# Normalising the last query block: one product that spreads each head's sum to all its rows, chunk by chunk, in place of a reciprocal of 16 columns, a transpose and four picking products

## The chip, the core and the metric

The kernel runs on one core of one Trainium2 chip. The core has five engines with a queue of instructions each: PE (TensorE, the matrix products), DVE (VectorE), ACT (ScalarE), POOL (GpSimd) and SP (SyncE, which here only issues transfers). They work beside each other and wait for one another through semaphores. The metric is the device time of one execution in microseconds (us), the median of several runs.

## What is computed

The input `A_x` has 2048 rows of 640 numbers. Two attention blocks, A and B, read the same input with weights of their own, and a sigmoid gate mixes their results row by row:

```
x = A_x
g = _sigmoid((x * gate_w).sum(-1, keepdims=True))
a = _A_ref(x, A_wqkv, A_wo)
b = _B_ref(x, B_wqkv, B_wo)
return g * a + (1 - g) * b
```

Each block projects x to queries, keys and values of 32 heads with 20 features each, takes the softmax of the scaled scores of 2048 queries against 2048 keys, weighs the values with it, and multiplies the 640 features with `wo`. What matters here is the last step of a softmax: the weighted values of each head and query have to be divided by that head's and query's sum of exponentials.

## The kernel before, in words

The heads are taken in groups of four, so there are 16 groups (8 of each attention block). For each group the 2048 queries are taken in 4 query blocks of 512, and for each query block the keys in 8 units of two times 128. That makes 512 steps, the loop at L1175. One step computes the scores of 128 keys by 512 queries for each of four heads (`scores`, L672), the exponentials of these on ACT (L675), and the products of the exponentials with the values, which add up in one PSUM bank, `acc` (`values`, L690). Beside that, a step carries products for the row maxima of later units (L614), projections, and the output product of features that are finished (`out_tiles`, L407 through `mms`).

Head h of the four has rows 32h to 32h+20 of `acc`: 20 rows of weighted values, and as row 32h+20 the sum, because the value tile has a column of ones (`DH` is 20). The columns of `acc` are the 512 queries. All other rows are zero, since `acc` is cleared once at the start (L867).

When the 8 units of a query block are done, `take_acc` (L773) empties `acc`, with transposes on DVE, a reciprocal of 16 columns, a product on POOL, and a split of the result into a half-precision part and a half-precision rest. It does this for 63 of the 64 query blocks, while PE goes on with the next one. The change does not touch it.

The last query block of the last group has nothing behind it. It is emptied by `take_last` (L811), called at L1214 after the loop. Before the change it goes like this:

1. ACT copies `acc` (128 rows by 512 queries) to a tile `ot` in SBUF (L814).
2. PE makes four products of 128 queries each (L818), with `ot` as the weights and four columns of the identity as the data: the sums come out turned, with queries as rows, in 16 columns of a PSUM bank.
3. DVE takes the reciprocal of these 16 columns (L820).
4. PE transposes them (L823), so that they have queries as columns, 16 rows of 128. ACT copies these to a tile `rt` (L825).
5. PE makes four more products (L829), with the tile `picks[0]` as the weights: each chooses the four rows of its 128 queries and repeats each over 32 rows. `picks[0]` was built by POOL in the last steps of the loop (`last_picks`, L805, L809).
6. For each of the four chunks of 128 queries, DVE multiplies `ot` by the reciprocals (L834), ACT casts the product to half precision (L835), and POOL takes the rest of it (L836).

Then `last_tiles` (L843) runs for the last query block, called at L1220. For each of the four chunks, and for each half of the 640 output columns, PE makes three products of 320 columns (L854): the half-precision part with the upper and the lower part of the weights, and the rest with the upper part. So there are 24 products in 8 groups of three. The groups of the first half, and both of the last chunk, are scaled and added to the output sums by DVE (L861). The second halves of chunks 0 to 2 are scaled by ACT (L857) and added by POOL (L858). Each chunk is then stored (L863), by SP's queue for chunks 0 and 2 and by ACT's queue for chunks 1 and 3.

What sets the order: the program is written under `tc.manual_schedule()`, so that each engine gets its instructions in the order in which the Python code issues them. `take` and `give` choose PSUM banks by a planned time at which each comes free (`spend`, `tick_block`); that plan chooses banks and moves nothing else here.

Of the kernel before, what the change touches and what calls it, by code (L numbers as in the profile page):

```python
# [11 lines left out]
F32 = mybir.dt.float32  # L12
I32 = mybir.dt.int32
AF = mybir.ActivationFunctionType
OP = mybir.AluOpType
# [4 lines left out]
P = 128  # L20
# [3 lines left out]
DH = 20  # L24
# [5 lines left out]
QB = 512  # L30
# [41 lines left out]
def kernel(  # L72
# [10 lines left out]
    nc = tc.nc  # L83
# [5 lines left out]
    wts = ctx.enter_context(tc.tile_pool(name="wts", bufs=2))  # L89
# [4 lines left out]
    ident = consts.tile([P, P], F32, name="ident")  # L94
# [15 lines left out]
    acc = psum.tile([P, QB], F32, name="acc")  # L110
# [24 lines left out]
    def take():  # L135

        i = min((k for k in range(NB) if k not in held), key=lambda k: free_at[k])
        held.add(i)
        return i, banks[i]

    def spend(engine, cost, ready=0.0):

        clock[engine] = max(clock[engine], ready) + cost
        return clock[engine] + T_BACK

    def give(i, t):
        free_at[i] = t
        held.discard(i)
# [93 lines left out]
    def scales_qk(i, maxima):  # L242

        return scales_by_dram(maxima, 2, lambda r, inv: set_qk(i, r, inv))
# [342 lines left out]
    def unit_of(u):  # L587
        gq, i = divmod(u, NS)
        g, qb = divmod(gq, NQ)
        return g, qb, i  # L590
# [212 lines left out]
    picks = []  # L803

    def last_picks():  # L805

        t = work.tile([P, QB], F32, name="fs")
        picks.append(t[:16].rearrange("p (k e) -> p k e", e=32))
        nc.gpsimd.tensor_copy(picks[0], ident[:16, :16].unsqueeze(2).to_broadcast([16, 16, 32]))  # L809

    def take_last():  # L811

        ot = work.tile([P, QB], F32, name="ot", bufs=2)
        nc.scalar.activation(ot, acc, AF.Copy)  # L814
        i, pt = take()
        one = ident.rearrange("p (h e) -> p h e", e=32)[:, :, DH]
        for t in range(4):
            nc.tensor.matmul(pt[:, 4 * t:4 * t + 4], ot[:, t * P:(t + 1) * P], one, start=True, stop=True)  # L818
        rc = work.tile([P, 16], F32, name="sq", bufs=2)
        nc.vector.reciprocal(rc, pt[:, :16])  # L820
        give(i, spend("dve", 0.3))
        i, pt = take()
        nc.tensor.transpose(pt[:16, :P], rc, ident)  # L823
        rt = wts.tile([16, P], F32, name="rt", tag="rt", bufs=1)
        nc.scalar.activation(rt, pt[:16, :P], AF.Copy)  # L825
        give(i, spend("act", 0.3))
        i, pt = take()
        for t in range(4):
            nc.tensor.matmul(pt[:, t * P:(t + 1) * P], picks[0].rearrange("p k e -> p (k e)")[:, t * P:(t + 1) * P], rt,  # L829
                             start=True, stop=True)  # L830
        o = work.tile([P, 2, QB], F16, name="on", bufs=2)
        for t in range(4):
            c = slice(t * P, (t + 1) * P)
            nc.vector.tensor_tensor(ot[:, c], ot[:, c], pt[:, c], op=OP.mult)  # L834
            nc.scalar.activation(o[:, 0, c], ot[:, c], AF.Copy)  # L835
            nc.gpsimd.tensor_tensor(o[:, 1, c], ot[:, c], o[:, 0, c], op=OP.subtract)  # L836
        give(i, spend("dve", 1.2, spend("act", T_EXP)))
        return o
# [30 lines left out]
    start = start_stack.enter_context(tc.tile_pool(name="start", bufs=1))  # L869
# [60 lines left out]
    for f in drains:  # L930
# [7 lines left out]
                            op=OP.subtract)  # L938
# [97 lines left out]
    work = ctx.enter_context(tc.tile_pool(name="work", bufs=2))  # L1036
# [18 lines left out]
    for g in range(2 * NG):  # L1055
        b = g * step
        n = g + 1
        if n < 2 * NG:
# [5 lines left out]
            i = g // 4 + 1  # L1064
            if i < 4:
                if g % 4 == 0:
                    z, c0 = i // 2, 320 * (i % 2)
                    srcs = max_tasks([[(wqkv[z], part * D + c0 + 160 * k) for k in range(2)] for part in range(2)],
                                     lambda m, i=i: scales_qk(i, m))
# [16 lines left out]
    for z in range(2):  # L1086
        parts = max_tasks([[(wo[z], 160 * k) for k in range(4)]], lambda m, z=z: scales_o(z, m), wrow[z])
        tasks(OMAX[z], 1, parts)
        for i in range(4):
            tasks(OSPLIT[z] + 3 * i, 2, out_weights(z, i))  # L1090
    at((2 * NG - 1) * step + 9, last_weights)
    at(STEPS - 4, last_picks)


# [80 lines left out]
    for G in range(STEPS + 1):  # L1175
        g, qb, i = unit_of(G)
# [12 lines left out]
        for what in (STEP[blocks] if maxima or some else LATE + " X" * (blocks == 2)).split():  # L1189
            k = count[what] = count.get(what, 0) + 1  # L1190
# [21 lines left out]
            else:  # L1212
                slot(G)
    end_o = take_last()  # L1214
    while side or parked or fill or current or outs or last:
        advance()
# [32 lines left out]
```

## Time and profile before

| what | value |
|---|---|
| device time, median of 3 runs | 2765.46 us (2764.1 to 2766.71) |
| device time of the profiled execution | 2765.39 us |
| its span (first to last event of the core) | 2763.6 us |
| mean granted clock of PE | 0.996 of full speed |
| busy time of ACT | 2525.4 us (91%) |
| busy time of DVE | 2441.0 us (88%) |
| busy time of POOL | 671.5 us (24%) |

The profile comes from one execution. Times in it are counted from the start of the span. A row of the timeline has its start, the time from its start to the end of the last instruction that it merges, the engine, the line of the code, the operation, what it writes and reads, the shapes (partitions by elements, type), how many instructions the row merges, and in brackets how long the engine sat idle before it and what ended that. PE counts matrix products, PEld the loading of their weights. A product of 32-bit numbers shows as two products and two loads in the trace. ACTq and SPq are transfers issued from the queues of ACT and SP. The chain of waits is followed back from the last work of the span.

### The profile page before, as it was taken

How to read it: one execution, taken by the hardware profiler on the slowest of the kernel's cores; microseconds unless marked ns; L12 is line 12 of the kernel's file. 1: busy time of each engine (PE TensorE's matmuls, PEld its weight loads, DVE VectorE, ACT ScalarE, POOL GpSimd, SP SyncE). 2: the span in 40 equal slices, each digit the busy share in tenths (PEclk: the TensorE clock that was granted, in tenths of full speed). 3: DMA queues.
4: the chain of work that ended last, by engine and by line, in shares of the span. 5: the costliest groups of instructions: out<-in, count | busy, mean ns of one | idle time of the engine just before them, and what ended most of it. 6: DMA issues, size and time to landing. Idle time of an engine off the chain costs nothing.

```text
span 2763.6 us, 62604 instructions
## 1 busy us (share of the span) xinstructions
PE 2725.5 (99%) x23453; PEld 938.0 (34%) x23453; DVE 2441.0 (88%) x4780; ACT 2525.4 (91%) x5140; POOL 671.5 (24%) x914
## 2 busy tenths in 40 slices
PE   7999999999999999999999999999999999999998
PEld 3433333333333332333333333333333333333222
DVE  7789999999999889888888998989988898999982
ACT  4999999999999999999999899999999999999997
POOL 6322223222123422311222111222342202100111
PEclk8999999999999999999999999999999999999999
DMA  4021102010120212102012230221201112122112
GB/s 142 17 57 26 31 11 47 8 31 16 25 55 20 60 35 56 41 9 61 20 41 66 60 84 26 60 56 48 65 16 42 30 50 63 32 77 64 47 47 76
DMA packets 176433, 125.60 MB, mean 45 GB/s; under 512 B 105216, under 2 KB 145976, under 8 KB 176128
## 3 DMA queue, kind: packets, MB, share of 16 engines
q1 hardware_dynamic: 173584, 119.99, 17.0%
q8 instruction: 183, 3.00, 0.5%
q0 software_dynamic: 1600, 0.96, 0.2%
q14 instruction: 122, 1.00, 0.1%
q10 hardware_dynamic: 944, 0.66, 0.1%
HBM read 55.53 MB, written 31.86 MB: 32 GB/s over the span
## 4 chain that ended last, share of the span: by engine, by line
PE 93%; DVE 4%; ACT 1%; DMA 1%; issue 0%; POOL 0%; SPq 0%; POOLq 0%; DVEq 0%; ACTq 0%
PE acc L690 35%; PE bank L407 20%; PE bank L614 20%; PE bank L672 18%; DVE mpart L625 2%; ACT pt L675 1%; DMA ws<-in_A_wqkv_dram 0%; DVE rl L622 0%; PE bank L854 0%; DVE ot L777 0%; DMA xs<-in_A_x_dram 0%; PE bank L900 0%; ACT rl L618 0%; DVE wmax L258 0%; DMA kd<-dd 0%
## 5 line engine op out<-in xcount | busy, mean ns | idle before, releaser
L675 ACT ACTIVATE pt<-bank 128x512 f32<-128x512 f32 x4096 | 2173.2, 615 | 147.9 <-PE bank L672 105.3
L625 DVE TENSOR_REDUCE mpart<-bank 128x1 f32<-128x512 f32 x2944 | 1842.4, 681 | 220.7 <-PE bank L614 117.4
L690 PE MATMUL acc<-pt,v 128*21 128x512 f32 x8192 | 1081.7, 600 | 0.7 <-DVE ot L777 0.6
L672 PE MATMUL bank<-qt,kt 64*128 64x512 f16 x4096 | 1039.1, 380 | 4.7 <-DVE mpart L625 2.7
L614 PE MATMUL bank<-kt,qt 60*128 60x512 f16 x3520 | 1010.6, 381 | 3.6 <-DVE mpart L625 1.0
L614 PEld LDWEIGHTS <-qt 60*128 60x128 f16 x4096 | 237.9, 94 | 906.8 <-issue 846.1
L622 DVE CUSTOM_DVE_ANT_0 rl<-bank,rl 128x512 f32<-128x512 f32 x576 | 386.7, 677 | 13.3 <-ACT rl L618 8.6
L618 ACT ACTIVATE rl<-bank 128x512 f32<-128x512 f32 x576 | 339.6, 600 | 11.9 <-PE bank L614 11.3
L407 PE MATMUL bank<-xx,wbh 128*128 128x168 f16 (+7 forms) x2600 | 291.4, 234 | 1.5 <-DVE wbh L926 1.0
L672 PEld LDWEIGHTS <-kt 64*128 64x128 f16 x4096 | 229.2, 94 | 178.8 <-issue 69.9
L690 PEld LDWEIGHTS acc<-pt,v 128*21 128x21 f32 x8192 | 143.0, 99 | 426.2 <-issue 421.9
L407 PE MATMUL bank<-xx,wbl 128*128 128x168 f16 (+7 forms) x1300 | 259.9, 232 | 0.0
L785 POOL TENSOR_TENSOR ot<-ot,sq 128x512 f32<-128x512 f32 x63 | 66.0, 1047 | 736.7 <-DVE sq L782 718.1
L407 PEld LDWEIGHTS <-wbh 128*128 128x128 f16 x2600 | 196.5, 98 | 118.4 <-issue 112.7
L614 PE MATMUL bank<-kd,qt 60*128 60x512 f16 x576 | 204.3, 380 | 2.3 <-DMA kd<-dd 2.2
L436 POOL CAST cq<-fs 128x512 f16<-128x512 f32 x60 | 36.6, 610 | 500.8 <-ACT fs L434 500.8
L407 PE MATMUL bank<-woh,o_in 128*128 128x320 f16 (+3 forms) x700 | 157.7, 290 | 0.0
L407 PE MATMUL bank<-wvh,xx 128*128 128x160 f16 (+1 forms) x1280 | 156.0, 234 | 0.0
L407 PEld LDWEIGHTS <-xx 128*128 128x128 f16 x1920 | 131.3, 97 | 56.1 <-issue 53.8
L407 PE MATMUL bank<-wvl,xx 128*128 128x160 f16 (+1 forms) x640 | 137.6, 232 | 0.0
L407 PEld LDWEIGHTS <-wbl 128*128 128x128 f16 x1300 | 127.4, 98 | 4.4 <-issue 1.3
L407 PEld LDWEIGHTS <-o_in 128*128 128x128 f16 (+1 forms) x1050 | 87.3, 97 | 90.7 <-issue 68.5
(140 smaller groups left out, 1251.8 us busy)
## 6 DMA issues: line engine op xcount, KB each, us to landing
y_scr<-y_out SPq DMA_DIRECT2D x48, 320.0 KB
y_out<-y_scr SPq DMA_DIRECT2D x32, 320.0 KB
kt<-cq SPq DMA_DIRECT2D x120, 80.0 KB
o_scr<-on SPq DMA_DIRECT2D x240, 40.0 KB
o_in<-o_scr SPq DMA_DIRECT2D x64, 96.0 KB
kt<-cq SPq DMA_DIRECT2D x136, 40.0 KB
wstage<-in_B_wqkv_dram SPq DMA_DIRECT2D x13, 400.0 KB
xs<-in_A_x_dram SPq DMA_DIRECT2D x8, 640.0 KB
```

Of the source, the lines that this page charges most:

```text
L407: nc.tensor.matmul(out_ap, a, b, start=(k == 0), stop=(k == len(pairs) - 1))
L436: nc.gpsimd.tensor_copy(hi, f)
L614: nc.tensor.matmul(pt, QT[g % 2][r, pair, q0:q0 + P], k, start=True, stop=True)
L618: nc.scalar.activation(relus[u, j], pt, AF.Relu)
L622: nc.vector.tensor_tensor_reduce(rl, pt, rl, 1.0, LOW, OP.add, OP.max, m)
L625: nc.vector.tensor_reduce(m, pt, axis=AX.X, op=OP.max)
L672: nc.tensor.matmul(et, KT[g % 2][r, pair, kt * P:(kt + 1) * P], QT[g % 2][r, pair, qb * QB:(qb + 1) * QB], start=True, stop=True)
L675: nc.scalar.activation(pt, et, AF.Exp, scale=factor(g // 4))
L690: nc.tensor.matmul(acc[32 * h:32 * h + VW, :], V[(g // 2) % 2][:, kt, (g % 2) * GH + h, :], ptiles.pop((G, kk, h)), start=(kt == 0), stop= ...
L785: nc.gpsimd.tensor_tensor(t3, t3, sq.unsqueeze(2).to_broadcast([P, 16, 32]), op=OP.mult)
```

## The change

`last_picks` builds another matrix: 128 by 128, with a one where the row is the sum's row of the head to which the column belongs. In `take_last`, one product with this matrix as the weights and a chunk of `ot` as the data then gives each head's sum in all the 32 rows of that head, with the queries still as columns. The reciprocal is taken after the product, over all 128 rows and 128 queries of the chunk. The products of L818, the transpose, the copy to `rt` and the picking products are gone. The copy of `acc`, the product, the reciprocal, the multiplication, the cast and the rest are all issued in one loop over the four chunks.

```diff
     def last_picks():
 
         t = work.tile([P, QB], F32, name="fs")
-        picks.append(t[:16].rearrange("p (k e) -> p k e", e=32))
-        nc.gpsimd.tensor_copy(picks[0], ident[:16, :16].unsqueeze(2).to_broadcast([16, 16, 32]))
+        picks.append(t[:, :P])
+        one = ident.rearrange("p (h e) -> p h e", e=32)[:, :, DH]
+        nc.gpsimd.tensor_copy(picks[0].rearrange("p (h e) -> p h e", e=32), one.unsqueeze(2).to_broadcast([P, 4, 32]))
 
     def take_last():
 
         ot = work.tile([P, QB], F32, name="ot", bufs=2)
-        nc.scalar.activation(ot, acc, AF.Copy)
         i, pt = take()
-        one = ident.rearrange("p (h e) -> p h e", e=32)[:, :, DH]
-        for t in range(4):
-            nc.tensor.matmul(pt[:, 4 * t:4 * t + 4], ot[:, t * P:(t + 1) * P], one, start=True, stop=True)
-        rc = work.tile([P, 16], F32, name="sq", bufs=2)
-        nc.vector.reciprocal(rc, pt[:, :16])
-        give(i, spend("dve", 0.3))
-        i, pt = take()
-        nc.tensor.transpose(pt[:16, :P], rc, ident)
-        rt = wts.tile([16, P], F32, name="rt", tag="rt", bufs=1)
-        nc.scalar.activation(rt, pt[:16, :P], AF.Copy)
-        give(i, spend("act", 0.3))
-        i, pt = take()
-        for t in range(4):
-            nc.tensor.matmul(pt[:, t * P:(t + 1) * P], picks[0].rearrange("p k e -> p (k e)")[:, t * P:(t + 1) * P], rt,
-                             start=True, stop=True)
+        rc = work.tile([P, QB], F32, name="ob", bufs=1)
         o = work.tile([P, 2, QB], F16, name="on", bufs=2)
         for t in range(4):
             c = slice(t * P, (t + 1) * P)
-            nc.vector.tensor_tensor(ot[:, c], ot[:, c], pt[:, c], op=OP.mult)
+            nc.scalar.activation(ot[:, c], acc[:, c], AF.Copy)
+            nc.tensor.matmul(pt[:, c], picks[0], ot[:, c], start=True, stop=True)
+            nc.vector.reciprocal(rc[:, c], pt[:, c])
+            nc.vector.tensor_tensor(ot[:, c], ot[:, c], rc[:, c], op=OP.mult)
             nc.scalar.activation(o[:, 0, c], ot[:, c], AF.Copy)
             nc.gpsimd.tensor_tensor(o[:, 1, c], ot[:, c], o[:, 0, c], op=OP.subtract)
         give(i, spend("dve", 1.2, spend("act", T_EXP)))
         return o
```

## The prediction

> **What bounds the kernel now.** I read the page first: the span, the busy shares and the shares of the chain that ended last.
>
> ```profile
> span 2763.6 us, 62604 instructions
> ...
> PE 2725.5 (99%) x23453; PEld 938.0 (34%) x23453; DVE 2441.0 (88%) x4780; ACT 2525.4 (91%) x5140; POOL 671.5 (24%) x914
> ...
> PE 93%; DVE 4%; ACT 1%; DMA 1%; issue 0%; POOL 0%; SPq 0%; POOLq 0%; DVEq 0%; ACTq 0%
> ```
>
> PE sets the time of the span as a whole. But the change touches only what comes after the last step of the loop, so I turned to the end of the chain of waits, in order of time.
>
> ```profile
> 2748.98 0.27 DVE sq L820
> ...
> 2749.30 0.29 PE bank L823
> ...
> 2749.61 0.27 ACT rt L825
> ...
> 2750.02 1.14 PE bank L829 x8
> ...
> 2751.25 0.30 DVE ot L834
> ...
> 2751.62 0.32 ACT on L835
> ```
>
> Here the chain hops from engine to engine, and PE only takes part. The timeline shows what stands around it (start, length, instruction).
>
> ```profile
> 2747.07 0.60 ACT L814 ACTIVATE ot<-acc 128x512 f32<-128x512 f32 x1 [1.75 <-PE acc L690]
> ...
> 2747.82 1.05 PE L818 MATMUL bank<-ident,ot 128*128 128x4 f32 x8
> 2748.00 0.55 DVE L758 SCALAR_TENSOR_TENSOR xx<-bank,f_o,xx 128x320 f32<-128x320 f32 x1 [1.47 <-PE bank L407]
> ...
> 2749.99 0.96 PEld L829 LDWEIGHTS bank<-rt,fs 16*128 16x128 f32 x8 [0.61 <-issue]
> ...
> 2751.25 0.88 DVE L834 TENSOR_TENSOR ot<-ot,bank 128x128 f32<-128x128 f32 x4 [2.01 <-PE bank L829]
> 2751.62 0.91 ACT L835 ACTIVATE on<-ot 128x128 f16<-128x128 f32 x4 [1.75 <-DVE ot L834]
> ...
> 2751.99 0.31 PE L854 MATMUL bank<-wbh,on 128*128 128x320 f16 x1 [0.84 <-ACT on L835]
> 2752.01 1.58 POOL L836 TENSOR_TENSOR on<-ot,on 128x128 f16<-128x128 f32 x4 [29.77 <-ACT on L835]
> ```
>
> From the start of the copy (2747.07) to the first of the 24 output products (2751.99) 4.92 us pass. From there to the end, these rows decide:
>
> ```profile
> 2755.38 0.53 ACT L857 ACTIVATE pt<-bank,f_o 128x320 f32<-128x320 f32 x1 [1.07 <-PE bank L854]
> ...
> 2755.99 0.87 POOL L858 TENSOR_TENSOR xx<-xx,pt 128x320 f32<-128x320 f32 x1 [0.74 <-ACT pt L857]
> ...
> 2756.88 0.36 ACTq L863 DMA_DIRECT2D out_dram<-xx  x1
> ...
> 2757.29 0.53 ACT L857 ACTIVATE pt<-bank,f_o 128x320 f32<-128x320 f32 x1 [1.38 <-PE bank L854]
> ...
> 2757.90 0.86 POOL L858 TENSOR_TENSOR xx<-xx,pt 128x320 f32<-128x320 f32 x1 [1.04 <-ACT pt L857]
> ```
>
> ACT works strictly in order: chunk 1's store (2756.88) waits for POOL's sum of chunk 1 (2755.99 + 0.87 = 2756.86), and the scaling of chunk 2 starts only behind it, at 2757.29. POOL's sum of chunk 2 ends at 2758.76, and its store is the last to go out. So the end hangs on when chunk 1's second group leaves PE.
>
> **Removed.** The products of L818, the reciprocal of 16 columns, the transpose, the copy to `rt` and the products of L829 are on the chain: from the first weights of L818 at 2747.82 to the first multiplication at 2751.25, 3.43 us. At most that can be won.
>
> **Added.** The four rounds go one after the other, because of ACT's queue: copy t+1 is written behind cast t, which waits for multiplication t, which waits for reciprocal t and product t. Queued behind the held cast is the next copy, and all of PE's output products wait for the fourth product. The prices:
>
> ```profile
> L836 POOL TENSOR_TENSOR on<-ot,on 128x128 f16<-128x128 f32 x4 | 1.6, 429 | 29.8 <-ACT on L835 29.8
> ...
> L434 ACT ACTIVATE fs<-bank 128x128 f32<-128x128 f32 x64 | 20.7, 324 | 0.0
> ...
> L782 DVE RECIPROCAL sq<-ot 128x16 f32<-128x16 f32 x63 | 16.0, 253 | 2.2
> ...
> L834 DVE TENSOR_TENSOR ot<-ot,bank 128x128 f32<-128x128 f32 x4 | 0.9, 281 | 2.0 <-PE bank L829 2.0
> ...
> L835 ACT ACTIVATE on<-ot 128x128 f16<-128x128 f32 x4 | 0.9, 298 | 1.7 <-DVE ot L834 1.7
> ...
> L233 DVE COPY r_v<-es 128x1 f32<-128x1 f32 x7 | 1.1, 154 | 0.0
> ```
>
> These are groups of instructions by line and shape; after the bar stand the busy time of all in us and the mean of one in ns.
>
> *The reciprocal of 128 columns* is the unknown; the trace has only 16 columns, 0.253 us. From below: if each further column costs what it costs L834 (0.281 for 128 columns against 0.154 for one, 1.0 ns a column), it takes 0.253 + 112 x 1.0 ns = 0.36 us. From above: eight times 0.253 = 2.02 us, if nothing of it is fixed. I take the fixed part from the copy of one column, the nearest row: (0.253 - 0.154) / 15 = 6.6 ns a column, so 0.253 + 112 x 6.6 ns = 0.99, say 1.0 us. The Trainium skill, VectorE: DVE Perf Modes, section on the walkthrough of the 8-slice pipeline, says that the reciprocal is an iterative divide with a repeat count of 8, and gives a clock of 0.96 GHz; eight cycles a column would make 1.07 us and a fixed part beside it, about 1.2 us as an estimate from that page, and the total would be 0.2 to 0.7 us longer than mine. The trace can't tell the two apart with one size.
>
> One round, then: copy 0.31 (between 0.298 and 0.324); to PE 0.11 (copy to `rt` ends 2749.88, next weights 2749.99); weights and two passes 0.45 (0.03 to the first pass; eight of L829 take 1.12, so 0.12 a pass and 0.28 for the last); to DVE 0.11 (2751.14 to 2751.25); reciprocal 1.0; gap and multiplication 0.03 + 0.28; to ACT 0.09; cast, of which the next copy waits for 0.20 (four casts: (0.91 - 0.30) / 3). That is 2.58 us. Does the copy also wait for POOL, which still reads another part of `ot`? Before, the fourth multiplication wrote `ot` at 2751.25 + 3 x 0.20 = 2751.85, ahead of POOL's first reading at 2752.01; so no.
>
> *Round 0.* The copy of the first chunk starts at 2747.07 as before and the product at 2747.82, behind the last L407 products. DVE has its own L758 in front until 2748.55, so reciprocal 0 starts at 2748.56, although its product has ended at 2748.27.
>
> *Rounds 1 to 3.* Reciprocals start at 2751.14, then 2753.72 and 2756.30 at full clock. But the clock falls, before as well:
>
> ```profile
> 2752.00:2753.00 1.00, 0.94 (x4) 0.38 (x5) 0.15 (x2) 0.53 (x3) 0.99 (x3) 0.70 0.00 0
> ...
> 2755.50:2756.00 0.50, 0.50 (x4) 0.31 (x3) 0.00 (x0) 0.41 (x1) 0.01 (x1) 0.69 0.00 0
> ```
>
> The seventh column of these two windows is the granted clock. Means of 0.70 and 0.69 between full and half put the fall at 2752.40 and the rise at 2755.81, a window of 3.41 us, after a stretch of sparse products. The 32-bit products of the start show what half clock costs:
>
> ```profile
> 25.88 1.06 PE L900 MATMUL bank<-ident,xs 128*128 128x128 f32 x4
> ...
> 28.94 0.60 PE L900 MATMUL bank<-ident,xs 128*128 128x128 f32 x4
> ```
>
> ```profile
> 26.90:28.60 1.70, 1.70 (x8) 1.17 (x6) 1.70 (x3) 1.23 (x3) 1.62 (x3) 0.51 0.00 0
> 28.60:30.31 1.71, 1.71 (x14) 1.29 (x12) 1.57 (x5) 1.37 (x2) 1.71 (x1) 1.00 0.00 0
> ```
>
> Four of them take 1.06 instead of 0.60, so a pair in rounds 2 and 3 costs about 0.18 more. Reciprocal 3 starts at 2756.30 + 0.36 = 2756.66, its product's weights at 2755.92, and the first output product can follow the second pass at about 2756.4, 4.4 us later than 2751.99.
>
> *The output products.* Now all of chunks 0 to 2 lies ready when they start, and PE runs without POOL's pace, at half clock:
>
> ```profile
> 2753.27 0.74 PE L854 MATMUL bank<-wbh,on 128*128 128x320 f16 x2
> ...
> 2754.07 0.74 PE L854 MATMUL bank<-wbh,on 128*128 128x320 f16 x2
> ...
> 2756.15 0.43 PE L854 MATMUL bank<-wbh,on 128*128 128x320 f16 x2
> ...
> 2756.56 0.43 PE L854 MATMUL bank<-wbh,on 128*128 128x320 f16 x2
> ```
>
> A group of three takes 0.80 us at half clock and 0.41 at full. Before, PE's products and POOL's first rests let chunk 1's second group reach ACT at 2755.38, 3.39 after the first product. Now four groups take 3.2 at half clock and 0.3 to drain and cross to ACT: 2759.9. If the clock rises at the next window's end (2755.81 + 3.41 = 2759.22), it is 2759.7. Meanwhile reciprocal 3 ends at 2757.66, cast 3 at 2758.36, the fourth rest at 2758.87, and POOL's sum of chunk 0 at 2759.73: none of this is later than chunk 1's group. POOL's sum of chunk 1 ends at 2759.7 + 0.53 + 0.08 + 0.87 = 2761.2, 4.3 us after 2756.86, and everything behind it follows as before. **The sum: +4.3 us**, so 2765.39 + 4.3 = 2769.7 us. The profiled execution lies 0.07 us from the median, so I need no correction.
>
> The new `picks[0]` costs nothing: POOL sits idle for 29.77 us ahead of L836, and without that cover it would be at most a fraction of a microsecond. No transfer is added or moved.
>
> The Trainium skill, TensorE: Matmul & The Clock Gate, section on the HAM clock gate, says that the 3.4 us window runs free and does not start with the kernel; then the fall and rise above lie elsewhere in another execution. The two rises in this trace fit: from 28.60 to 2755.81 are 799.0 of the page's windows of 3413 ns. One execution can't show the phase of another. By rows, with a rise anywhere, chunk 1's group comes between 0.5 us sooner and 0.2 us later, so the sum would be +3.8 to +4.5.
>
> **The rivals.**
>
> *Slower by over 0.2%: the reciprocal has no fixed part to speak of.* Place: DVE in each round. Three reciprocals lie ahead of the first output product and the fourth ahead of POOL's sums, so every 0.1 us of it costs 0.3 to 0.4 us. At 2.02 us the fourth rest ends 4.1 us later, at 2762.95, and two sums, the store, the scaling and the last sum end at 2766.6: +7.8 us, 2773.2. It decides from about 1.4 us on, where the total passes 5.5 us. For it speaks that the one size shows nothing fixed; against it that 0.15 us are spent on a single column. Rounds that are 0.4 us longer through other waits would end the same way.
>
> *The reciprocal streams.* At 0.36 us three rounds shrink by 1.9 us: output products from 2754.5, chunk 1's group at 2758.0, +2.6 us, 2768.0. For it: all other rows of DVE run at about a column per ns. Against: 16 columns of any other kind would take 0.17, not 0.253.
>
> *The rounds overlap after all,* if the copies are not held behind the casts. Then all products are done by 2748.9, reciprocal and multiplication follow at 1.31 us a round, the fourth rest ends at 2754.8, and POOL's three sums with the store between them end at about 2758.4: -0.4 us, 2765.0. For it: the products need nothing from the casts. Against: the code's order, and ACT's wait at 2756.88 to 2757.29, which shows the order kept. This is also the case in which the change does what its words say.
>
> **How the numbers follow.** A measurement of this kernel can tell about 0.2%, 5.5 us, from no change. Chances: the forecast with 0.9 to 1.35 us for the reciprocal 0.67; streaming 0.10; overlapping rounds 0.06; a long reciprocal or longer rounds 0.17. Even all that is removed (3.43 us) is less than 5.5 us, so faster by over 0.2% has 0.01 for the measurement; slower has the last rival and a part of the forecast's upper end, 0.24; the rest, 0.75, is within. The range goes from 2767.3 (streaming, less half the spread of the three runs) to 2772.0 (reciprocal of about 1.5 us with rounds as summed); beyond it lie most of the overlapping case and about half of the long reciprocal, some 0.16.
>
> **What would show it.** The timeline after should have copies, pairs of products, reciprocals, multiplications and casts in four steps about 2.6 us apart, each copy right behind the cast before it; DVE's reciprocal near 1.0 us; the first output product near 2756.4; PE's clock at half during the first of these; the sum of chunk 1 ending near 2761.2. I am wrong if the four copies stand close together, if the reciprocal lies far from 1.0, or if the output products start before the fourth product.

## The result, and the profile after

The median of 22 runs is 2769.86 us (2767.39 to 2771.9), against 2765.37 us before (22 runs, 2763.44 to 2767.71). The ratio is 1.0017, 95% interval 1.0011 to 1.0022: 4.5 us slower, clear of noise. That is within the 0.2% (5.5 us) that the prediction took as the least that can be told from no change; with 22 runs of each kernel the interval is narrower than that. The profiled execution took 2769.29 us, with a span of 2767.5 us.

The timeline after, with only the first of PE's output products (start, length, engine and line, instruction, idle time before it). L820 is now the copy, L821 the product, L822 the reciprocal, L823 the multiplication, L824 the cast, L825 the rest.

```profile
2746.62 0.28 ACT L820 ACTIVATE ot<-acc 128x128 f32<-128x128 f32 x1 [1.75 <-PE acc L690]
...
2748.02 0.95 DVE L822 RECIPROCAL ob<-bank 128x128 f32<-128x128 f32 x1
2749.07 0.29 DVE L823 TENSOR_TENSOR ot<-ot,ob 128x128 f32<-128x128 f32 x1
2749.45 0.31 ACT L824 ACTIVATE on<-ot 128x128 f16<-128x128 f32 x1 [2.55 <-DVE ot L823]
2749.66 0.26 ACT L820 ACTIVATE ot<-acc 128x128 f32<-128x128 f32 x1
...
2749.98 0.49 PE L821 MATMUL bank<-ot,fs 128*128 128x128 f32 x2 [2.12 <-ACT ot L820]
2750.50 0.96 DVE L822 RECIPROCAL ob<-bank 128x128 f32<-128x128 f32 x1 [1.14 <-PE bank L821]
...
2752.42 0.80 PE L821 MATMUL bank<-ot,fs 128*128 128x128 f32 x2 [1.96 <-ACT ot L820]
2753.26 0.96 DVE L822 RECIPROCAL ob<-bank 128x128 f32<-128x128 f32 x1 [1.40 <-PE bank L821]
...
2755.76 0.47 PE L843 MATMUL bank<-wbh,on 128*128 128x320 f16 x1
2756.00 0.96 DVE L822 RECIPROCAL ob<-bank 128x128 f32<-128x128 f32 x1 [1.39 <-PE bank L821]
```

Copy 1 starts at 2749.66, behind cast 0 at 2749.45, although `acc` was ready at 2746.62. The reciprocals start 2.48, 2.76 and 2.74 us apart. The first output product starts 9.14 us after the first copy; before it was 4.92. The rows that lead to the end:

```profile
2759.26 0.53 ACT L846 ACTIVATE pt<-bank,f_o 128x320 f32<-128x320 f32 x1 [1.07 <-PE bank L843]
...
2759.87 0.86 POOL L847 TENSOR_TENSOR xx<-xx,pt 128x320 f32<-128x320 f32 x1 [0.74 <-ACT pt L846]
...
2760.76 0.36 ACTq L852 DMA_DIRECT2D out_dram<-xx  x1
...
2761.22 0.53 ACT L846 ACTIVATE pt<-bank,f_o 128x320 f32<-128x320 f32 x1 [1.43 <-PE bank L843]
...
2761.83 0.86 POOL L847 TENSOR_TENSOR xx<-xx,pt 128x320 f32<-128x320 f32 x1 [1.10 <-ACT pt L846]
```

They have the shape of before: sum of chunk 1, store from ACT, scaling and sum of chunk 2. The last sum ends at 2762.69.

The first copy of `acc` starts between 2746.0 and 2748.3 us in the profiled executions of this study, though the change does not touch the steps ahead of it; what moves it was not looked into. So I compare the *tail*, from the start of the first copy of `acc` to the end of POOL's last sum: 2758.76 - 2747.07 = 11.69 us before, 2762.69 - 2746.62 = 16.07 after, +4.38 us. Of these, 4.22 us have gathered by the first output product (9.14 - 4.92).

### The profile page after: what moved, and what is told of

It reads as the page before. It is cut to its first block, busy times and chain, and to the rows that moved or that the text cites. A ratio compares the mean times of both kernels' runs of the same rounds, so it can differ in the third digit from the quotient of the medians.

```text
span 2767.5 us, 62596 instructions
## 1 busy us (share of the span) xinstructions
PE 2725.4 (98%) x23444; PEld 938.0 (34%) x23444; DVE 2445.7 (88%) x4783; ACT 2526.0 (91%) x5142; POOL 671.9 (24%) x914
## 4 chain that ended last, share of the span: by engine, by line
PE 93%; DVE 4%; ACT 1%; DMA 1%; issue 1%; POOL 0%; SPq 0%; POOLq 0%; DVEq 0%; ACTq 0%
PE acc L690 35%; PE bank L407 20%; PE bank L614 20%; PE bank L672 18%; DVE mpart L625 2%; ACT pt L675 1%; DVE rl L622 0%; DMA ws<-in_A_wqkv_dram 0%; PE bank L843 0%; DVE ot L777 0%; PE bank L889 0%; DMA xs<-in_A_x_dram 0%; DVE wmax L258 0%; DVE ob L822 0%; ACT rl L618 0%
```

## The experiments

**Theory:** ACT's order holds the rounds one behind another, and each step of a round, the reciprocal of 128 columns above all, counts three times before PE's first output product. **Rival D:** the length of four reciprocals decides, in whatever order. **Rival C:** PE's clock, at half for longer, decides.

| kernel | first copy, last sum ends | tail, us | median, us | ratio to before, 95% interval |
|---|---|---|---|---|
| before | 2747.07, 2758.76 | 11.69 | 2765.37 | |
| changed | 2746.62, 2762.69 | 16.07 | 2769.86 | 1.0017 (1.0011 to 1.0022) |
| copies first | 2747.44, 2759.07 | 11.63 | 2765.47 | 0.9998 (0.9989 to 1.0007) |
| constant | 2748.22, 2761.97 | 13.75 | 2767.55 | 1.0007 (0.9998 to 1.0016) |
| reciprocal twice | 2746.54, 2765.90 | 19.36 | 2772.83 | 1.0026 (1.0016 to 1.0037) |
| copies first, constant | 2746.65, 2755.62 | 8.97 | 2763.34 | 0.9992 (0.9983 to 1.0001) |
| filler | 2747.37, 2761.96 | 14.59 | 2768.46 | 1.0010 (1.0001 to 1.0019) |
| banks | 2747.33, 2759.00 | 11.67 | 2763.74 | 0.9994 (0.9985 to 1.0003) |
| direct | 2746.04, 2755.74 | 9.70 | 2764.44 | 0.9995 (0.9986 to 1.0004) |
| direct, store on SP | 2748.24, 2757.89 | 9.65 | 2763.21 | 0.9988 (0.9979 to 0.9997) |
| direct, store on SP, filler | 2748.02, 2756.27 | 8.25 | 2762.11 | 0.9986 (0.9977 to 0.9995) |

Medians beside the ratios are of 8 to 22 runs; the ratio is to runs of the kernel before on the same chip (2765.53 us for the four kernels after the changed one, 2765.72 for the next four, 2765.84 for the last). Each of the nine intervals below the changed kernel's is about 5 us wide, so they do not part two of these kernels whose medians lie 1 to 3 us from each other; that takes their timelines, each of one execution.

### The order undone

```diff
         for t in range(4):
             c = slice(t * P, (t + 1) * P)
             nc.scalar.activation(ot[:, c], acc[:, c], AF.Copy)
             nc.tensor.matmul(pt[:, c], picks[0], ot[:, c], start=True, stop=True)
+        for t in range(4):
+            c = slice(t * P, (t + 1) * P)
             nc.vector.reciprocal(rc[:, c], pt[:, c])
```

> The four copies of acc and the four products are issued ahead of all reciprocals, multiplications, casts and rests; nothing else differs from the changed kernel. Theory (the rounds are held one behind another by ACT's order, so copy, product, reciprocal, multiplication and part of the cast count three times before the first output product): the products end within about 1.2 us, only DVE's reciprocal and multiplication repeat (about 1.3 us a chunk), the first output product starts near 3.4 us after the first copy instead of 9.1, and the time falls by about 4.5 us to 2765.4 us, level with the kernel before. Rival D (the length of four reciprocals of 128 columns decides, in whatever order): DVE still has about 5 us to do, the time stays near 2768.9. Rival C (the longer stretch of half clock on PE decides): the products between stay as sparse, near 2768.5 to 2769.5.

Measured: 2765.47 us. The timeline of this kernel (L824 reciprocal, L825 multiplication):

```profile
2748.19 1.16 PE L821 MATMUL bank<-ot,fs 128*128 128x128 f32 x8
2749.44 0.96 DVE L824 RECIPROCAL ob<-bank 128x128 f32<-128x128 f32 x1 [0.52 <-PE bank L821]
2750.50 0.29 DVE L825 TENSOR_TENSOR ot<-ot,ob 128x128 f32<-128x128 f32 x1
2750.71 0.95 DVE L824 RECIPROCAL ob<-bank 128x128 f32<-128x128 f32 x1
...
2751.24 0.31 PE L845 MATMUL bank<-wbh,on 128*128 128x320 f16 x1 [1.89 <-ACT on L826]
```

The reciprocals are as long as in the changed kernel, but now 1.27 us apart, and the first output product comes 3.80 us after the first copy. The whole loss is gone by the order alone. D had said 2768.9 and falls. C had said 2768.5 at the least and falls too: the profile has PE at half clock again in the middle of the tail (granted clock 0.50 from 2751.8 to 2755.1), and the loss was gone. The first output product comes 1.12 us sooner than in the kernel before (3.80 against 4.92), but the tail is only 0.06 us shorter: the fourth cast, at 2754.62 behind the fourth reciprocal, stands in ACT's queue ahead of the first scaling of output products, at 2754.84.

### The reciprocal made short, and made double

```diff
-            nc.vector.reciprocal(rc[:, c], pt[:, c])
+            nc.vector.tensor_scalar(rc[:, c], pt[:, c], 0.0, 0.0005, op0=OP.mult, op1=OP.add)
```

> Order of the changed kernel kept; each reciprocal is replaced by one DVE instruction of the same shape, from PSUM to SBUF, that writes a constant (the normalisation of the last query block is left out). Theory: that instruction takes about 0.25 us instead of 0.96, the round falls from 2.5 to 1.8 us, three rounds lie ahead of the first output product: about 2.1 us less, 2767.8 us, still above the kernel before. Rival D: four times 0.7 us and nothing else was the loss, 2766.5 or below. Rival C: 2769.5, since PE is as idle as before.

Measured: 2767.55 us. The constant takes 0.28 us, rounds are 1.8 us (2.1 in the one at half clock), and the first output product starts 6.82 us after the first copy, 2.32 sooner than in the changed kernel; the tail is 2.32 shorter. The theory had said 2767.8. The interval, 2765.0 to 2770.0 us, also holds what D (2766.5 or below) and C (2769.5) said; it is the timeline, with the 2.32 us all won ahead of the first output product, that bears the theory out. In the timeline (L822 is the constant):

```profile
2749.61 0.28 DVE L822 TENSOR_SCALAR ob<-bank 128x128 f32<-128x128 f32 x1
...
2751.43 0.29 DVE L822 TENSOR_SCALAR ob<-bank 128x128 f32<-128x128 f32 x1 [1.14 <-PE bank L821]
...
2753.20 0.29 DVE L822 TENSOR_SCALAR ob<-bank 128x128 f32<-128x128 f32 x1 [1.09 <-PE bank L821]
...
2755.04 0.47 PE L843 MATMUL bank<-wbh,on 128*128 128x320 f16 x1
```

```diff
             nc.vector.reciprocal(rc[:, c], pt[:, c])
+            nc.vector.reciprocal(rc[:, c], pt[:, c])
```

> Each reciprocal of the changed kernel is issued twice, in the same place. Theory: 0.96 us more in each round, three ahead of the first output product and a fourth ahead of POOL's sums: +2.9 to +3.8 us, 2772.8 to 2773.7 us. Rival C: PE was idle at half clock anyway, +1 us or less. Rival D: +3.8 us, so D and the theory are not told apart here.

Measured: 2772.83 us, 3.0 us over the changed kernel, 3.29 by the tail: three times 0.96 and a little. C, with 1 us or less, falls here. The two runs give one price from both sides: the kernel changes by three to three and a half times the change of the one step.

### Both

```diff
             nc.tensor.matmul(pt[:, c], picks[0], ot[:, c], start=True, stop=True)
-            nc.vector.reciprocal(rc[:, c], pt[:, c])
+        for t in range(4):
+            c = slice(t * P, (t + 1) * P)
+            nc.vector.tensor_scalar(rc[:, c], pt[:, c], 0.0, 0.0005, op0=OP.mult, op1=OP.add)
```

> Both edits: copies and products first, and the constant in place of the reciprocals (the normalisation of the last query block is left out). Theory: a chunk costs DVE about 0.6 us, the first output product starts about 2.5 us after the first copy, POOL's rests and sums and PE's products set the end: 2762.0 to 2763.0 us, under the kernel before. Rival D: equal to the run with the constant alone, 2766.5. Rival C: no lower than 2767, because PE still falls to half clock.

Measured: 2763.34 us, a little over the expected range; the interval of the ratio includes 1. D (2766.5) falls, since the interval ends at 2765.8. C isn't tested by this run: in the profiled execution the clock stayed full through the tail. The tail of 8.97 us is 2.66 shorter than with copies first and the reciprocals kept. Here the four rests and the sums on POOL follow the first cast closely, and ACT's wait for the store of chunk 1 is what remains: POOL sits idle for 1.10 us before the sum of chunk 2, which starts at 2754.76.

### PE kept busy

```diff
+        k, dummy = take()
...
             nc.tensor.matmul(pt[:, c], picks[0], ot[:, c], start=True, stop=True)
+            if t < 3:
+                for _ in range(12):
+                    nc.tensor.matmul(dummy[:, :320], wo_parts[2][0][:, :P], wo_parts[2][0][:, :320], start=True, stop=True)
...
+        give(k, spend("dve", 0.1))
```

> The changed kernel, with twelve 320-column half-precision products of no use behind each of the first three 32-bit products, into a bank that nothing reads, so that PE isn't sparse and its clock should stay full. Theory (the rounds decide): the rounds keep their 2.48 us, the two pairs at half clock win 0.6 us back, the output products run at 0.41 a group instead of 0.80; then POOL's rests and sums decide, and the last sum ends 1.4 us sooner: 2768.5 us. Rival C (the longer half clock is the loss): back to 2766 or less. No change at all (2769.9) if the clock falls all the same.

Measured: 2768.46 us. Windows of the whole tail of this kernel; the seventh column is the granted clock:

```profile
2748.00:2752.00 4.00, 3.52 (x26) 2.40 (x25) 2.46 (x4) 0.47 (x2) 0.42 (x1) 1.00 0.00 0
2752.00:2756.00 4.00, 3.35 (x24) 2.17 (x22) 1.74 (x4) 0.95 (x4) 0.85 (x2) 1.00 0.00 0
2756.00:2760.00 4.00, 3.51 (x25) 2.17 (x23) 3.33 (x7) 1.14 (x3) 2.10 (x3) 1.00 0.00 0
```

With PE at full clock throughout, 1.4 us of the 4.5 come back (1.48 by the tail), and the rounds stay at 2.44 to 2.48 us. C (2766 or less) is at best at the edge of the interval, and the tail, still 2.90 us longer than before, speaks against it: the clock has a share, but the larger one is that of the rounds. How much filler would win the kernel before, which has 3.41 us at half clock itself, wasn't tried, so the 1.4 us are not all loss of the change.

### A wait for the bank, and a shorter middle

The picking products of the kernel before were put in four banks, one for each chunk, and the multiplications read them from there:

```diff
-        i, pt = take()
+        four = [take() for t in range(4)]
         for t in range(4):
-            nc.tensor.matmul(pt[:, t * P:(t + 1) * P], picks[0].rearrange("p k e -> p (k e)")[:, t * P:(t + 1) * P], rt,
+            nc.tensor.matmul(four[t][1][:, :P], picks[0].rearrange("p k e -> p (k e)")[:, t * P:(t + 1) * P], rt,
...
-            nc.vector.tensor_tensor(ot[:, c], ot[:, c], pt[:, c], op=OP.mult)
+            nc.vector.tensor_tensor(ot[:, c], ot[:, c], four[t][1][:, :P], op=OP.mult)
...
```

> The kernel before, with its four picking products in four PSUM banks instead of one. Its first multiplication started only after all eight passes (2751.25) though its own pair was done near 2750.44. If that wait is for the whole bank, the first multiplication starts 0.65 us sooner and the time falls to 2764.8 us; copies_first showed the same wait (its first reciprocal started after the eighth pass). If the wait is of another kind, nothing changes: 2765.4.

```profile
2750.27 2.01 PE L829 MATMUL bank<-rt,fs 16*128 16x128 f32 x8 [0.45 <-ACT rt L825]
2751.04 1.14 DVE L834 TENSOR_TENSOR ot<-ot,bank 128x128 f32<-128x128 f32 x3 [1.55 <-PE bank L829]
```

The first multiplication (2751.04) now starts while the picking products run on until 2752.28, so the wait was for the bank as a whole. Whether the program or the chip imposes it wasn't tried. The median, 2763.74 us, lies below both forecasts (2764.8 and 2765.4), but the total can't be told from no change: the ratio's interval includes 1. The profiled tail is the same as before (11.67); in that execution the clock fell at 2750.3, ahead of most of these products, which took 2.01 us in place of 1.12.

Then a shorter middle with short reciprocals kept, `ident` as the data:

```diff
-        i, pt = take()
-        nc.tensor.transpose(pt[:16, :P], rc, ident)
...
+        wide = work.tile([P, QB], F32, name="ob", bufs=1)
+        four = [take() for t in range(4)]
         for t in range(4):
...
+            nc.vector.tensor_copy(wide[:, t * P:(t + 1) * P].rearrange("p (h e) -> p h e", e=32),
+                                  rc[:, 4 * t:4 * t + 4].unsqueeze(2).to_broadcast([P, 4, 32]))
+            nc.tensor.matmul(four[t][1][:, :P], wide[:, t * P:(t + 1) * P], ident, start=True, stop=True)
...
-            nc.vector.tensor_tensor(ot[:, c], ot[:, c], pt[:, c], op=OP.mult)
+            nc.vector.tensor_tensor(ot[:, c], ot[:, c], four[t][1][:, :P], op=OP.mult)
...
```

> The kernel before with a shorter middle: the 16 reciprocals are spread by DVE over 32 columns each (four copies of 128 columns, about 0.2 us each), and one product per chunk with them as weights and the identity as data turns and spreads them at once, each into a bank of its own; the transpose, the copy to rt and the picking product are gone. Theory (the chain of hops ahead of the first output product sets the end, short reciprocals kept): the first multiplication starts about 1.0 us sooner, 2764.4 us, and 2763.0 if the stretch of sparse PE gets short enough to keep the clock. Rival (PE's 24 products and the tail of ACT and POOL behind them set the end anyway): 2765.4.

Measured: 2764.44 us, as expected, though the interval includes 1. The first multiplication comes 3.14 us after the first copy (2749.18 - 2746.04) instead of 4.18. The profiled execution kept full clock, and took 2762.36. POOL still sits idle ahead of its last sum:

```profile
2754.88 0.86 POOL L849 TENSOR_TENSOR xx<-xx,pt 128x320 f32<-128x320 f32 x1 [1.05 <-ACT pt L848]
```

The store of chunk 1 was then moved from ACT's queue to SP's:

```diff
-            (nc.scalar if qb == NQ - 1 and t % 2 else nc.sync).dma_start(out_t[:, 4 * qb + t, :], y_sum[:, 4 * qb + t])
+            (nc.scalar if qb == NQ - 1 and t == 3 else nc.sync).dma_start(out_t[:, 4 * qb + t, :], y_sum[:, 4 * qb + t])
```

> The run before this one, with the store of chunk 1 issued by SP's queue instead of ACT's, so that the scaling of chunk 2 on ACT isn't held behind a transfer that waits for POOL. If that hold is on the path, POOL's three sums follow each other without a gap and the end comes about 1.0 us sooner than in the run without it: 2762.0 to 2763.4 us. If the last store is late for another reason, no change against it.

Measured: 2763.21 us, ratio 0.9988, interval 0.9979 to 0.9997: faster than the kernel before, by a little, and than the changed one. POOL's sums of chunks 1 and 2 now stand in one row without a gap:

```profile
2756.21 1.68 POOL L849 TENSOR_TENSOR xx<-xx,pt 128x320 f32<-128x320 f32 x2 [0.32 <-ACT pt L848]
```

So the hold by the store is gone. What it won in time this run alone does not show: the interval overlaps that of the run without it, and the profiled tail is 9.65 against 9.70 us, since this execution had PE at half clock from 2750.8 to 2754.2 and the other did not. The next run, at full clock, has a tail to compare.

```diff
+        k, dummy = take()
+        for _ in range(4):
+            nc.tensor.matmul(dummy[:, :320], wo_parts[2][0][:, :P], wo_parts[2][0][:, :320], start=True, stop=True)
+        give(k, spend("dve", 0.1))
         wide = work.tile([P, QB], F32, name="ob", bufs=1)
```

> The run with the shorter middle and chunk 1's store on SP, with four 320-column products of no use (0.54 us at full clock) behind the products that turn the sums, where PE waits about 0.9 us for DVE. The eleven times of the run without them fall into two heaps (2760.3 to 2761.4 and 2763.0 to 2764.5), and its profiled execution, of the upper heap, shows PE at half clock from 2750.9 to 2754.1. If the heaps are executions in which the clock stays full and in which it falls, more of the executions land in the lower heap: median 2761 us. If PE's clock isn't what parts them, or half a microsecond isn't enough to hold it: 2763.2 us as without.

Measured: 2762.11 us, ratio 0.9986, interval 0.9977 to 0.9995; it isn't told apart from the run before this one (2763.21). The profiled execution, 2762.88 us, kept full clock through the tail of 8.25 us. That is 1.45 us less than the 9.70 of the shorter middle with the store on ACT, also at full clock: in both, POOL's first sum starts 5.75 us after the first copy, but the idle stretches of 0.32 and 1.05 us between its sums are gone, and the longer one was the wait behind the store.

The eleven times run evenly from 2760.97 to 2763.67, without two heaps. In the run before this one the mean granted clock of an execution parts the heaps (0.997 in all four of the lower, 0.995 or 0.996 in all seven of the upper), which speaks for the clock. Here 0.997 goes with times from 2760.97 to 2763.67, and the profiled execution, at full clock in the tail, did not take a time of the lower heap. What made two heaps stays open.

### The reciprocal by itself

```diff
+    rs = start.tile([P, 2, QB], F32, name="rs")
+    nc.vector.memset(rs[:, 0], 1.0)
+    for n in (1, 32, 64, 128, 256, 512):
+        nc.vector.reciprocal(rs[:, 1, :n], rs[:, 0, :n])
```

> The changed kernel with six reciprocals of 1, 32, 64, 128, 256 and 512 columns on 128 rows on DVE, from SBUF to SBUF, at the start. From the two sizes so far (0.253 us for 16 columns, 0.956 for 128: 6.3 ns a column and 0.153 us fixed) they should take 0.16, 0.35, 0.56, 0.96, 1.76 and 3.37 us. If the reciprocal had no fixed part, 512 would take four times the 128. The time of the whole is of no interest here; DVE is held some 7 us at the start.

The groups by line and shape of this kernel (busy time in us and the mean of one in ns behind the bar):

```profile
L879 DVE RECIPROCAL rs<-rs 128x512 f32<-128x512 f32 x1 | 3.4, 3353 | 0.0
L879 DVE RECIPROCAL rs<-rs 128x256 f32<-128x256 f32 x1 | 1.8, 1753 | 0.0
L879 DVE RECIPROCAL rs<-rs 128x128 f32<-128x128 f32 x1 | 1.0, 953 | 0.0
L879 DVE RECIPROCAL rs<-rs 128x64 f32<-128x64 f32 x1 | 0.6, 553 | 0.0
L879 DVE RECIPROCAL rs<-rs 128x32 f32<-128x32 f32 x1 | 0.4, 354 | 0.0
...
L879 DVE RECIPROCAL rs<-rs 128x1 f32<-128x1 f32 x1 | 0.2, 164 | 0.0
```

From 256 to 512 columns it is 1.600 us for 256, 6.25 ns a column, over some 0.15 us fixed.

## Why the prediction was right

- *The rounds one after another.* Shown: copy 1 stands behind cast 0, and with the order undone the loss is gone. The prediction's rival of overlapping rounds gave 2765.0 for an order that the changed kernel doesn't have; the kernel that has it took 2765.47.
- *The reciprocal at 1.0 us.* It took 0.956. The fixed part taken from the copy of one column (0.154) was right to 0.01 us, and 6.6 ns a column was 6.25. The Trainium skill, VectorE: DVE Perf Modes, has a repeat count of 8 for the reciprocal, in the section on the walkthrough of the 8-slice pipeline, and a clock of 0.96 GHz, in the section of specifications; 6.25 ns are six cycles of that clock, so the estimate of eight cycles a column, which would have made the total up to 0.7 us longer, is not what was measured here. The measurement decides.
- *The round at 2.58 us.* It was 2.48: the copy took 0.26 and not 0.31, the reciprocal was 0.05 shorter, and the hand-overs from ACT to PE and from PE to DVE took 0.05 and 0.03 and not 0.11 each. Against these, the multiplication started 0.10 behind the reciprocal and not 0.03, and the pair of products took 0.49 and not 0.45.
- *The rounds at half clock, 0.18 more each.* Mis-sized: they were 0.28 and 0.26 longer, mostly since a pair took 0.80 us and not the 0.49 of full clock. The prediction's own rows give 0.23 for a pair, half of 1.06 - 0.60, so 0.18 was too small from the start. That took back more than half of what the shorter rounds gave: the first output product came 9.14 us after the first copy, for which the prediction had 2756.4 - 2747.07 = 9.3.
- *The clock's return at the next window's end.* The clock fell at 2750.68 in this execution and came back at 2760.92, three windows later: not at the end of the first window in which output products ran, but of the next one. That rounds 2 and 3 were the ones at half clock, as in the sum, is partly luck: the pair of round 1 ended at 2750.47, 0.2 us ahead of the fall.

```profile
2754.09:2757.51 3.42, 2.34 (x9) 1.58 (x10) 1.82 (x5) 0.60 (x3) 0.43 (x1) 0.50 0.00 0
2757.51:2760.92 3.41, 3.41 (x15) 1.91 (x13) 1.41 (x3) 1.21 (x3) 2.15 (x3) 0.50 0.25 96
```

  PE was busy for 2.34 us (second number) in the window after which the clock stayed at half, and for 3.41 in the one after which it rose. The busy share alone is not the rule: in the run with four banks PE was busy for 3.41 of 3.41 us from 2750.31 to 2753.72, and the clock came back only at 2757.13. Chunk 1's group needed 3.50 us from the first output product to ACT's scaling, where the sum had 3.3 with a rise and 3.5 without.
- *Chunk 1's sum and what follows.* It ended 2760.73 - 2746.62 = 14.11 us after the first copy; the prediction had 2761.2 - 2747.07 = 14.13. What followed kept its shape, with the store of chunk 1 ahead of the scaling of chunk 2 in ACT's queue.
- *The sum, +4.3 us.* The tail is +4.38 and the medians differ by 4.49. The closeness to the predicted time owes something to chance: terms were off by 0.1 to 0.3 us both ways. The range does not come out as it was worked out: 2768.0 less half the spread of the three runs, 1.3 us, is 2766.7 and not 2767.3. The measured 2769.86 lies well inside either.

## What to carry to other kernels

A loop that issues copy, product, reciprocal and cast chunk by chunk pipelines nothing if its first and its last step are on one engine that keeps its order: look for the engine that stands at both ends of the body, and issue its early steps for all chunks first. A reciprocal costs by columns here, six times what a multiplication costs (6.25 measured against 1.0 ns a column, the prediction's estimate from L834), so it belongs where the values stand in few columns over many rows. And at the end of a kernel look for a store that waits in the queue of an engine which still has work: moved to an idle queue, it let the work behind it go on, and the 1.05 us that POOL had been idle ahead of its last sum were gone.

## What the runs showed of the hardware that was not expected

A reader on DVE of one quarter of a PSUM bank started only when PE had finished with all four quarters (2751.25 before, with the first pair done near 2750.44), and not with a bank for each quarter (2751.04, with PE at work until 2752.28). Whether the program or the chip makes it wait is not shown. PE's clock did not come back after a window with PE busy for 2.34 of 3.42 us, nor, with four banks, after one with 3.41 of 3.41 us, though in the kernel before it did after one with 3.35. So a late burst of products can run at half clock for longer than one window of 3.41 us, and what decides is open.
